# Attention backward on one core: E is transposed in groups of six in every step, and the dK/dV matmuls move to step 19, behind those transposes

## The chip, the core and the metric

The kernel runs on one core of a Trainium2 chip. The metric is device time in microseconds (us) for one execution. Before the change three runs took 2691.83, 2700.37 and 2707.21 us, so the median is 2700.37 us.

## The reference

The reference computes one block `x + s * g` and all its gradients. There, `s` is multi-head attention on a normalised `x` (32 heads of 16 channels, 2048 tokens), and `g` is a gated channel MLP. Only the attention matters for this change:

```python
xn  = layernorm(A_x)
q, k, v = split_heads(xn @ wqkv)            # 32 heads, 16 channels, 2048 tokens
p   = softmax(q k^T / 4)                    # 2048 x 2048 for every head
o   = p v ;  s = o @ wo
out = x + s * silu(mlp(xn))
grads = vjp(out, grad_out)                  # of A_x, A_wqkv, A_wo and the MLP's weights
```

The backward pass of the attention needs, for every head, dV = P^T dO, dS = P * (dO V^T - rowsum), dQ = dS K and dK = dS^T Q. The kernel never stores P. It computes E = exp(scores - bound) once, and G = (V dO^T) * E, and corrects for the softmax's sum and for the row sums afterwards.

## The kernel before

The program has three phases: layer norms, projections and MLP forward (`phase_pre`), the attention with its backward pass (`attention_core`, about 284 to 2084 us of the profiled span), and the remaining gradients (`phase3`). The change touches only `attention_core`.

**Tiling.** Heads are taken in 16 pairs, and queries in four chunks `qc` of 512, which makes 64 blocks. A block has 16 steps `kb`, one for every 128 keys. There are thus 1024 steps, numbered g, and a loop of 24 more to drain. "Step 10" below means g mod 16 = 10. A queue order is written out by hand: every engine executes its instructions in the order in which the body of the loop over g emits them (`tc.manual_schedule()`).

**What one step does**, with the tile names that the profile uses:

- `emit_s(g + 1, hj)`: scores `s` of the next step, one matmul for each head of the pair (L629), and on ScalarE their exponential into the tile `et` (L635), which holds E with keys on the partitions, four steps to a tile.
- `emit_d(g, hj)`: the products `d` of V and dO (L647).
- `emit_mult(g)`: on VectorE, `gts` = `d` times `et`, which is G (L660), two instructions of 128x512.
- `emit_x(g - 1, "l" / "e" / "g")`: six narrow matmuls into the accumulator `X` (L719, L722, L725): sums of E, E against K and V, and G against ones and K.
- `emit_dmat(g)`: DMA transposes on SyncE's queue (SP). In every second step one turns `gts` into `gk` (queries on the partitions), and in every fourth one turns a quarter of `et` (the query sub-block `qb` = 3 of four steps) into `ek`.
- `emit_T` and `emit_cT`: the other three quarters of E. In 12 of 16 steps TensorE transposes eight 128x128 blocks of an `et` tile that was completed earlier into the PSUM tile `tT` (L694), and ScalarE copies them to `ek` (L704).
- `emit_z` and `emit_acc`: four matmuls of 32 output rows into the accumulator `Z`, which becomes dK and dV of 1024 keys (L804). Their stationary operands `W1`, `W2` hold corrected Q and dO. A block has 16 such units, one a step; they run from the 21st step after its first (`ZOFF = -21`), eight for each half of the keys. After eight units the half is added to `acc` by VectorE (L817 for the first query chunk, L819 for the others). This falls on steps 12 and 4.
- Once in a block: `emit_xs` copies `X` to SBUF on ScalarE (L734) in step 0 of the next block. `emit_XT` transposes it in fp32 on TensorE (L744) and `emit_fin` (VectorE L756 to L770, then GpSimd) makes `W1`, `W2`, O and dQ of it in step 2 (`FIN_AT = 2`).

**Order in a step.** TensorE gets `Z`, the first `s`, (`XT` in step 2), both `d`, the second `s`, `tT`, and the `X` matmuls of the step before. ScalarE gets two exponentials, (`xs` in step 0), and the copy of `tT`. VectorE gets (`acc`), the two products, (`fin`).

**Buffers.** `s` and `tT` share a ring of three PSUM banks (`ps_st`), `d` and `XT` another of three (`ps_d`). `X` and `Z` have one bank each. In SBUF there are three tiles of `et`, three of `gts`, seven of `gk` and nineteen of `ek`. A matmul into a ring's bank waits until the reader of the bank's last content has finished.

Of the kernel before, what the change touches and what calls it, by code (L numbers as in the profile page):

```python
# [8 lines left out]
bf16 = mybir.dt.bfloat16  # L9
f32 = mybir.dt.float32  # L10
# [532 lines left out]
def attention_core(ctx, tc, NAT_s, NATQ_s, Oall, dQall, dKVT_out, ident_f32, ident_bf, npairs=16, nqc=4):  # L543
    nc = tc.nc
# [5 lines left out]
    ps_z = ctx.enter_context(tc.tile_pool(name="ps_z", bufs=1, space=PSUM))  # L550
    etp = sb("etp", 3)
    gtp = sb("gtp", 3)
    gbp = sb("gbp", 7)
    ekp = sb("ekp", 19)
    xsp = sb("xsp", 1)
    finp = sb("finp", 1)
    wp = sb("wp", 2)
# [49 lines left out]
    cur = {}  # L607

    def a_unit(g):
        return (g // 16, g % 16) if 0 <= g < NSTEP else None  # L610
# [53 lines left out]
    def emit_dmat(g):  # L664
        a = a_unit(g)
        if a is None:
            return
        j, kb = a
        kc = kb // 4
        if kb % 2 == 1:  # L670
            h = (kb // 2) % 2
            if h == 0:
                blk[j]["Gk"][kc] = gbp.tile([128, 2, 16, 128], bf16, name="gk")
            nc.sync.dma_start_transpose(out=blk[j]["Gk"][kc][:, h], in_=st_gt[g][:].rearrange("k a h q -> k (a h q)"))
        if kb % 4 == 3:
            ek = ekp.tile([128, 8, 128], bf16, name="ek")
            blk[j]["Ek"][(kc, 3)] = ek
            nc.sync.dma_start_transpose(out=ek[:], in_=st_et[g][:, 3].rearrange("k a h q -> k (a h q)"))

    def t_unit(g):  # L680
        a = a_unit(g - 4)
        if a is None or a[1] % 4 == 3:
            return None
        return a[0], a[1] // 4, a[1] % 4

    def emit_T(g):
        u = t_unit(g)
        if u is None:
            return
        j, kc, qb = u  # L690
        et = st_et[j * 16 + kc * 4 + 3]
        t = ps_st.tile([128, 8, 128], bf16, name="tT", tag="st")
        for b in range(8):
            nc.tensor.transpose(t[:, b, :], et[:, qb, b // 2, b % 2, :], ident_bf[:])  # L694
        st_T[g] = t

    def emit_cT(g):
        u = t_unit(g)
        if u is None:
            return  # L700
        j, kc, qb = u
        ek = ekp.tile([128, 8, 128], bf16, name="ek")
        blk[j]["Ek"][(kc, qb)] = ek
        nc.scalar.copy(out=ek[:].rearrange("q a k -> q (a k)").bitcast(f32),  # L704
                       in_=st_T.pop(g)[:].rearrange("q a k -> q (a k)").bitcast(f32))

    def emit_x(g, part):
        a = a_unit(g)
# [19 lines left out]
    def emit_xs(g):  # L728
        a = a_unit(g)
        if a is None or a[1] != 15:  # L730
            return
        j = a[0]
        xs = xsp.tile([128, 512], f32, name="xs")
        nc.scalar.copy(out=xs[:], in_=blk[j].pop("X")[:])  # L734
        blk[j]["xs"] = xs

# [10 lines left out]
    def emit_fin(g):  # L747
        j = g // 16 - 1
        if g % 16 != FIN_AT or not 0 <= j < NB:
            return  # L750
        p, qc = blocks[j]
        NQq = op_of(j)["NATQq"]
        NQd = op_of(j)["NATQd"]
        XT = blk[j].pop("XT")
        xt = finp.tile([128, 4, 128], f32, name="xt")
        nc.vector.tensor_copy(out=xt[:], in_=XT[:])  # L756
        XTv = xt[:].rearrange("q b (r c) -> q b r c", r=4)
        W1 = wp.tile([128, 4, 2, 32], bf16, name="W1")
        W2 = wp.tile([128, 4, 2, 32], bf16, name="W2")
        nc.gpsimd.memset(W2[:, :, :, 0:16], 0.0)  # L760
        st0 = qc * 4
        nqs = NQq[:, st0:st0 + 4, :, 1:17]
        ndo = NQd[:, st0:st0 + 4, :, :]
        bc = lambda ap: ap.to_broadcast([128, 4, 2, 16])
        rL = finp.tile([128, 4, 2, 1], f32, name="rL")
        nc.vector.reciprocal(out=rL[:], in_=XTv[:, :, 2:4, 17:18])  # L766
        dl = finp.tile([128, 4, 2, 1], f32, name="dl")
        nc.vector.tensor_tensor(out=dl[:], in0=XTv[:, :, 2:4, 0:1], in1=rL[:], op=ALU.mult)
        ndr = finp.tile([128, 4, 2, 1], f32, name="ndr")
        nc.vector.scalar_tensor_tensor(out=ndr[:], in0=dl[:], scalar=-1.0, in1=rL[:], op0=ALU.mult, op1=ALU.mult)  # L770
        nc.gpsimd.tensor_tensor(out=W2[:, :, :, 16:32], in0=nqs, in1=bc(rL[:]), op=ALU.mult)  # L771
        nc.gpsimd.tensor_tensor(out=W1[:, :, :, 0:16], in0=ndo, in1=bc(rL[:]), op=ALU.mult)
        nc.gpsimd.tensor_tensor(out=W1[:, :, :, 16:32], in0=nqs, in1=bc(ndr[:]), op=ALU.mult)
        Ov = Oall[:, st0:st0 + 4, p * 32:(p + 1) * 32].rearrange("q b (h c) -> q b h c", h=2)
        nc.gpsimd.tensor_tensor(out=Ov, in0=XTv[:, :, 0:2, 16:32], in1=bc(rL[:]), op=ALU.mult)
        t1 = finp.tile([128, 4, 2, 16], f32, name="t1")
        nc.gpsimd.tensor_tensor(out=t1[:], in0=XTv[:, :, 0:2, 0:16], in1=bc(dl[:]), op=ALU.mult)
        nc.gpsimd.tensor_tensor(out=t1[:], in0=XTv[:, :, 2:4, 1:17], in1=t1[:], op=ALU.subtract)
        rL4 = finp.tile([128, 4, 2, 1], f32, name="rL4")
        nc.gpsimd.tensor_scalar(out=rL4[:], in0=rL[:], scalar1=0.25, scalar2=None, op0=ALU.mult)  # L780
        dQv = dQall[:, st0:st0 + 4, p * 32:(p + 1) * 32].rearrange("q b (h c) -> q b h c", h=2)
        nc.gpsimd.tensor_tensor(out=dQv, in0=t1[:], in1=bc(rL4[:]), op=ALU.mult)
        blk[j]["W1"] = W1
        blk[j]["W2"] = W2

    def emit_z(g):
        u = z_unit(g)
        if u is None:
            return
        j, kp, qb, part = u  # L790
        if part == 0 and qb == 0:
            blk[j]["Z"] = ps_z.tile([128, 512], f32, name="Z", tag="z")
        Z = blk[j]["Z"]
        for par in range(2):
            kc = 2 * kp + par
            if part == 0:
                W = blk[j]["W2"]
                mv = blk[j]["Gk"][kc][:].rearrange("q a (r h b) k -> q h b a r k", r=2, h=2)[:, :, qb]
            else:
                W = blk[j]["W1"]  # L800
                mv = blk[j]["Ek"].pop((kc, qb))[:].rearrange("q (a h) k -> q h a k", h=2)
            for hj in range(2):
                r = 64 * par + 32 * hj
                nc.tensor.matmul(Z[r:r + 32, :], lhsT=W[:, qb, hj, :], rhs=mv[:, hj],  # L804
                                 start=(part == 0 and qb == 0), stop=(part == 1 and qb == 3), skip_group_check=True,
                                 tile_position=(0, r))

    def emit_acc(g):
        u = z_unit(g)
        if u is None or u[2] != 3 or u[3] != 1:  # L810
            return
        j, kp = u[0], u[1]
        p, qc = blocks[j]
        Z = blk[j]["Z"]
        av = acc[:, kp, :]
        if qc == 0:
            nc.vector.tensor_copy(out=av, in_=Z[:])  # L817
        else:
            nc.vector.tensor_tensor(out=av, in0=Z[:], in1=av, op=ALU.add)  # L819
        if qc == nqc - 1:  # L820
            if kp == 0:
                cur["ob"] = outp.tile([128, 2, 512], bf16, name="ob")
            ob = cur["ob"]
            nc.gpsimd.tensor_copy(out=ob[:, kp, :], in_=av)
            if kp == 1:
                def store():
                    dv = dKVT_out[p * 64:(p + 1) * 64, :].rearrange("r (a b s) -> r a b s", a=2, b=2)
                    for b in range(2):
                        nc.sync.dma_start(out=dv[:, :, b, :], in_=ob[b * 64:(b + 1) * 64])
                late.append((cur["g"] + 2, store))  # L830

    FIN_AT = 2
    ZOFF = -21
    late = []
    for f in load_ops(0):
        f()
# [2 lines left out]
    for g in range(NSTEP + 16 + 8):  # L839
        cur["g"] = g  # L840
        a = a_unit(g)
        if a is not None:
            j, kb = a
            p, qc = blocks[j]
            if kb == 0 and qc == 1 and p + 1 < npairs:
                for i, f in enumerate(load_ops(p + 1)):
                    late.append((g + 1 + 4 * i, f))
        for it in [x for x in late if x[0] <= g]:
            late.remove(it)
            it[1]()  # L850
        emit_z(g + ZOFF)
        emit_acc(g + ZOFF)
        emit_s(g + 1, 0)
        emit_XT(g)
        emit_d(g, 0)
        emit_d(g, 1)
        emit_s(g + 1, 1)
        emit_mult(g)
        emit_fin(g)
        emit_T(g)  # L860
        emit_x(g - 1, "l")
        emit_x(g - 1, "e")
        emit_x(g - 1, "g")
        emit_xs(g - 1)
        emit_cT(g)
        emit_dmat(g)
        st_gt.pop(g - 2, None)
        st_et.pop(g - 12, None)
# [104 lines left out]
```

## Time and profile before

| | |
|---|---|
| median of three runs | 2700.37 us (2691.83 to 2707.21) |
| the profiled execution: time, span | 2689.98 us, 2688.2 us |
| mean granted TensorE clock | 0.957 of full speed |
| share of the span busy: PE, VectorE, ScalarE, GpSimd | 85%, 71%, 67%, 22% |
| in the attention (284 to 2084 us): PE, VectorE, ScalarE, GpSimd | 1702.7, 1433.8, 1529.8, 249.3 us of 1800 |
| granted clock and DMA share in that stretch | 1.00, 1.08 |
| transposes `tT` (L694) | 6144, 475.2 us busy |
| copies of `tT` (L704) | 768, 455.2 us busy, mean 593 ns |

The page lists busy time by engine (PE is TensorE's matmuls, PEld its weight loads, DVE is VectorE, ACT ScalarE, POOL GpSimd, SP SyncE). Matmuls are pipelined: each is shown for some 0.38 us here, though the next may begin 0.22 us after it or at the same time, so a busy engine is not one at its peak. More is learned from the timeline, which gives the start and length of every instruction, and in brackets how long its engine had been idle and what ended that. A DMA share above 1 means that several packets overlap on an engine.

### The profile page before, as it was taken

What the parts mean: (1) busy time and instruction counts of PE and PEld (TensorE: products, weight loads), DVE (VectorE), ACT (ScalarE), POOL (GpSimd) and SP (SyncE); (2) the same over time, 40 slices, a digit from 0 to 9 for tenths busy, and PEclk for the clock granted to TensorE, in tenths of its full rate; (3) what the DMA queues carried; (4) which work ended last, traced back from release to release, by engine and by line L of the source; (5) the groups of instructions that cost most, each with busy time, mean ns of one, the idle gap of its engine ahead of it and who ended that gap; (6) DMA issues with size and microseconds to landing.
All of it is one profiled execution on the core that took longest, in us unless ns stands there. A gap on an engine that the chain in (4) does not pass through costs nothing. (4 is left out here: it accounts for less than half of the span.)

```text
span 2688.2 us, 61100 instructions
## 1 busy us (share of the span) xinstructions
PE 2294.1 (85%) x24005; PEld 1054.0 (39%) x24064; DVE 1898.4 (71%) x3190; ACT 1795.7 (67%) x3317; POOL 600.7 (22%) x990
## 2 busy tenths in 40 slices
PE   3788799999999999999999999999999656656967
PEld 2333244444444444444444444444444333322433
DVE  5766687878788778787787877778787368860144
ACT  3344688888888888888888888888887254430110
POOL 0434111011110111101111011110111258850034
PEclk8899899999999999999999999999999878878989
DMA  5343999999999999999999999999999633327331
GB/s 188 94 128 126 186 199 212 195 211 204 204 216 193 211 204 204 215 196 215 201 202 215 191 214 202 205 209 198 210 198 182 229 109 103 103 72 185 116 111 43
DMA packets 1564740, 477.08 MB, mean 177 GB/s; under 512 B 1484706, under 2 KB 1549603, under 8 KB 1564451
## 3 DMA queue, kind: packets, MB, share of 16 engines
q1 hardware_dynamic: 1491058, 419.56, 78.5%
q10 hardware_dynamic: 73392, 53.62, 6.5%
q8 instruction: 188, 3.08, 0.5%
q14 instruction: 102, 0.83, 0.1%
HBM read 65.41 MB, written 55.32 MB: 45 GB/s over the span
## 5 line engine op out<-in xcount | busy, mean ns | idle before, releaser
L660 DVE TENSOR_TENSOR gts<-d,et 128x512 bf16<-128x512 f32 x2048 | 1292.3, 683 | 364.1 <-PE s L629 200.1
L635 ACT ACTIVATE et<-s 128x512 bf16<-128x512 f32 x2048 | 1127.3, 596 | 247.9 <-PE s L629 136.7
L629 PE MATMUL s<-QDT,KVT 32*128 32x512 bf16 x2048 | 528.0, 386 | 17.7 <-DMA QDT<-Pad 16.1
L647 PE MATMUL d<-QDT,KVT 32*128 32x512 bf16 x2048 | 489.9, 383 | 54.0 <-DVE gts L660 53.7
L694 PE MATMUL tT<-ident_bf,et 128*128 128x128 bf16 x6144 | 475.2, 220 | 40.1 <-ACT ek L704 39.4
L704 ACT COPY ek<-tT 128x512 f32<-128x512 f32 x768 | 455.2, 593 | 0.5 <-PE tT L694 0.5
L694 PEld LDWEIGHTS <-et 128*128 128x128 bf16 x6144 | 354.2, 98 | 213.1 <-issue 199.2
L722 PE MATMUL X<-et,NAT 128*32 128x512 bf16 x2048 | 404.0, 392 | 0.0
L719 PE MATMUL X<-et,Lc 128*32 128x512 bf16 x2048 | 403.4, 391 | 0.0
L725 PE MATMUL X<-gts,NAT 128*17 128x512 bf16 x2048 | 393.4, 380 | 0.0
L629 PEld LDWEIGHTS <-KVT 32*128 32x128 bf16 x2048 | 145.3, 91 | 555.1 <-issue 523.8
L804 PE MATMUL Z<-ek,W 128*32 128x512 bf16 x2048 | 300.8, 380 | 0.0
L804 PE MATMUL Z<-gk,W 128*32 128x512 bf16 x2048 | 289.6, 380 | 1.3 <-DVE acc L819 1.3
L771 POOL TENSOR_TENSOR W<-NATQq,rL 128x128 bf16<-128x128 bf16 x64 | 25.7, 401 | 1178.3 <-DVE rL L766 1178.3
L804 PEld LDWEIGHTS <-W 128*32 128x32 bf16 x4096 | 199.7, 96 | 125.9 <-issue 31.2
L719 PEld LDWEIGHTS <-Lc 128*32 128x32 bf16 x2048 | 98.2, 93 | 139.0 <-issue 59.6
L647 PEld LDWEIGHTS <-KVT 32*128 32x128 bf16 x2048 | 96.0, 91 | 11.4 <-issue 11.4
L722 PEld LDWEIGHTS <-NAT 128*32 128x32 bf16 x2048 | 98.6, 93 | 0.0
L421 PE MATMUL dh_tp<-ident_bf,dh 128*128 128x128 bf16 x224 | 31.0, 278 | 77.9 <-DVE dh L418 75.5
L725 PEld LDWEIGHTS <-NAT 128*17 128x17 bf16 x2048 | 95.3, 90 | 0.0
L448 PE MATMUL ps_dw<-dm_all,hgc 128*128 128x512 bf16 x220 | 54.0, 402 | 29.6 <-DMA hgc<-HG_s 29.4
L427 PE MATMUL ps_dy<-w1T,dh1T 128*128 128x512 bf16 x208 | 67.8, 471 | 3.7 <-ACT dh1T L422 3.4
(197 smaller groups left out, 2442.2 us busy)
## 6 DMA issues: line engine op xcount, KB each, us to landing
gk<-gts SPq DMA_TRANSPOSE x512, 4.2
HG_s<-hg SPq DMA_DIRECT2D x16, 448.0 KB, 2.9
DH_s<-dh ACTq DMA_DIRECT2D x16, 448.0 KB, 2.5
NAT<-NAT_s SPq DMA_DIRECT2D x16, 264.0 KB, 3.3
GB_s<-gB ACTq DMA_DIRECT2D x16, 256.0 KB, 2.0
ek<-et SPq DMA_TRANSPOSE x256, 3.1
dKVT_s<-ob SPq DMA_DIRECT2D x32, 128.0 KB, 2.5
dhc<-DH_s ACTq DMA_DIRECT2D x2, 2048.0 KB, 13.7
```

The costliest lines, as they stand in the source:

```text
L427: nc.tensor.matmul(ps[:], lhsT=dh1T[:, fc, :], rhs=w1T[:, fc, :], start=(fc == 0), stop=(fc == FC - 1))
L448: nc.tensor.matmul(ps[:], lhsT=hgc[:, t, :], rhs=dm_all[:, t, :], start=(t == 0), stop=(t == NT - 1))
L629: nc.tensor.matmul(s[:], lhsT=op["KVT"][r:r + 32, kb * 128:(kb + 1) * 128], rhs=op["QDT"][r:r + 32, qc * 512:(qc + 1) * 512], start=True, ...
L635: nc.scalar.activation(out=et[:, :, kb % 4, hj, :], in_=s[:].rearrange("k (b q) -> k b q", b=4), func=ACT.Exp)
L647: nc.tensor.matmul(d[:], lhsT=op["KVT"][r:r + 32, kb * 128:(kb + 1) * 128], rhs=op["QDT"][r:r + 32, qc * 512:(qc + 1) * 512], start=True, ...
L660: nc.vector.tensor_tensor(out=gts[:, kb % 2, hj, :].rearrange("k (b q) -> k b q", b=4), in0=st_d.pop((g, hj))[:].rearrange("k (b q) -> k b ...
L694: nc.tensor.transpose(t[:, b, :], et[:, qb, b // 2, b % 2, :], ident_bf[:])
L704: nc.scalar.copy(out=ek[:].rearrange("q a k -> q (a k)").bitcast(f32), in_=st_T.pop(g)[:].rearrange("q a k -> q (a k)").bitcast(f32))
L719: nc.tensor.matmul(X[64 + 32 * hj:96 + 32 * hj, :], lhsT=Lc[:], rhs=et[:, :, kb % 4, hj, :], start=(kb == 0), stop=False, skip_group_check ...
L722: nc.tensor.matmul(X[32 * hj:32 * hj + 32, :], lhsT=NATt[:, kb, hj, 1:33], rhs=et[:, :, kb % 4, hj, :], start=(kb == 0), stop=(kb == 15), ...
L725: nc.tensor.matmul(X[64 + 32 * hj:64 + 32 * hj + 17, :], lhsT=NATt[:, kb, hj, 0:17], rhs=st_gt[g][:, kb % 2, hj, :], start=False, stop=(kb ...
L804: nc.tensor.matmul(Z[r:r + 32, :], lhsT=W[:, qb, hj, :], rhs=mv[:, hj], start=(part == 0 and qb == 0), stop=(part == 1 and qb == 3), skip_ ...
```

## The change

Three things change in `attention_core`, with the buffers that they need.

1. The transposes. In all 16 steps of a block TensorE transposes six 128x128 blocks of E, those of the current step (three query sub-blocks of both heads), instead of eight blocks of an older tile in 12 of 16 steps. ScalarE copies 128x384 words each time. One `ek` tile of four steps is filled by four such copies.
2. The order. `Z` is no longer first in the step. It stands behind the transposes, and in step 1 behind `XT`, and before the `X` matmuls. `XT` moves from between `s` and `d` to behind the transposes. dK/dV of a block begin at its step 19 instead of 21, so `acc` falls on steps 10 and 2, and `fin` is done in step 1 instead of 2.
3. Buffers: `gk` six tiles instead of seven, `ek` six small (from the DMA) and six large (from ScalarE) instead of nineteen small, and `xt` uses the buffer of `xs`. The output tile `ob` is stored after each half instead of after both, in stores of half the size.

```diff
-    gbp = sb("gbp", 7)
-    ekp = sb("ekp", 19)
+    gbp = sb("gbp", 6)
+    ekd = sb("ekd", 6)
+    ekc = sb("ekc", 6)
...
-    def t_unit(g):
-        a = a_unit(g - 4)
-        if a is None or a[1] % 4 == 3:
-            return None
-        return a[0], a[1] // 4, a[1] % 4
...
     def emit_T(g):
-        u = t_unit(g)
-        if u is None:
-            return
-        j, kc, qb = u
-        et = st_et[j * 16 + kc * 4 + 3]
-        t = ps_st.tile([128, 8, 128], bf16, name="tT", tag="st")
-        for b in range(8):
-            nc.tensor.transpose(t[:, b, :], et[:, qb, b // 2, b % 2, :], ident_bf[:])
+        a = a_unit(g)
+        if a is None:
+            return
+        kk = a[1] % 4
+        et = st_et[g]
+        t = ps_st.tile([128, 3, 2, 128], bf16, name="tT", tag="st")
+        for qb in range(3):
+            for hj in range(2):
+                nc.tensor.transpose(t[:, qb, hj, :], et[:, qb, kk, hj, :], ident_bf[:])
         st_T[g] = t
 
     def emit_cT(g):
...
-        ek = ekp.tile([128, 8, 128], bf16, name="ek")
-        blk[j]["Ek"][(kc, qb)] = ek
-        nc.scalar.copy(out=ek[:].rearrange("q a k -> q (a k)").bitcast(f32),
-                       in_=st_T.pop(g)[:].rearrange("q a k -> q (a k)").bitcast(f32))
+        if kk == 0:
+            cur["ek"] = ekc.tile([128, 3, 4, 2, 128], bf16, name="ek")
+            blk[j]["Ek"][kc] = cur["ek"]
+        nc.scalar.copy(out=cur["ek"][:, :, kk].rearrange("q b h k -> q b (h k)").bitcast(f32),
+                       in_=t[:].rearrange("q b h k -> q b (h k)").bitcast(f32))
...
-        xs = xsp.tile([128, 512], f32, name="xs")
+        xs = xsp.tile([128, 512], f32, name="xs", tag="xs")
...
-        xt = finp.tile([128, 4, 128], f32, name="xt")
+        xt = xsp.tile([128, 4, 128], f32, name="xt", tag="xs")
...
-    FIN_AT = 2
-    ZOFF = -21
+    FIN_AT = 1
+    ZOFF = -19
...
-        emit_z(g + ZOFF)
-        emit_acc(g + ZOFF)
         emit_s(g + 1, 0)
-        emit_XT(g)
         emit_d(g, 0)
         emit_d(g, 1)
         emit_s(g + 1, 1)
+        emit_T(g)
+        emit_XT(g)
+        emit_z(g + ZOFF)
+        emit_acc(g + ZOFF)
         emit_mult(g)
         emit_fin(g)
-        emit_T(g)
         emit_x(g - 1, "l")
```

More of the change, by code (lines that the diff above doesn't have):

```diff
@@ L675, in emit_dmat @@
         if kb % 4 == 3:
-            ek = ekp.tile([128, 8, 128], bf16, name="ek")
+            ek = ekd.tile([128, 4, 2, 128], bf16, name="ekd")
             blk[j]["Ek"][(kc, 3)] = ek
-            nc.sync.dma_start_transpose(out=ek[:], in_=st_et[g][:, 3].rearrange("k a h q -> k (a h q)"))
-    def t_unit(g):
-        a = a_unit(g - 4)
-        if a is None or a[1] % 4 == 3:
-            return None
-        return a[0], a[1] // 4, a[1] % 4
+            nc.sync.dma_start_transpose(out=ek[:].rearrange("q a h k -> q (a h) k"), in_=st_et[g][:, 3].rearrange("k a h q -> k (a h q)"))
     def emit_T(g):
-        u = t_unit(g)
-        if u is None:
+        a = a_unit(g)
+        if a is None:
             return
-        j, kc, qb = u
-        et = st_et[j * 16 + kc * 4 + 3]
-        t = ps_st.tile([128, 8, 128], bf16, name="tT", tag="st")
-        for b in range(8):
-            nc.tensor.transpose(t[:, b, :], et[:, qb, b // 2, b % 2, :], ident_bf[:])
+        kk = a[1] % 4
[4 more added lines that the diff above has]
+                nc.tensor.transpose(t[:, qb, hj, :], et[:, qb, kk, hj, :], ident_bf[:])
         st_T[g] = t
     def emit_cT(g):
-        u = t_unit(g)
-        if u is None:
+        a = a_unit(g)
+        if a is None:
             return
-        j, kc, qb = u
-        ek = ekp.tile([128, 8, 128], bf16, name="ek")
-        blk[j]["Ek"][(kc, qb)] = ek
-        nc.scalar.copy(out=ek[:].rearrange("q a k -> q (a k)").bitcast(f32),
-                       in_=st_T.pop(g)[:].rearrange("q a k -> q (a k)").bitcast(f32))
+        j, kb = a
+        kc, kk = kb // 4, kb % 4
+        t = st_T.pop(g)
+        if kk == 0:
[3 more added lines that the diff above has]
+                       in_=t[:].rearrange("q b h k -> q b (h k)").bitcast(f32))
     def emit_x(g, part):
@@ L800, in emit_z @@
                 W = blk[j]["W1"]
-                mv = blk[j]["Ek"].pop((kc, qb))[:].rearrange("q (a h) k -> q h a k", h=2)
+                mv = blk[j]["Ek"][(kc, 3)][:] if qb == 3 else blk[j]["Ek"][kc][:, qb]
+                mv = mv.rearrange("q a h k -> q h a k")
             for hj in range(2):
@@ L820, in emit_acc, with store @@
         if qc == nqc - 1:
[L821 to L830, printed above, removed]
-    FIN_AT = 2
-    ZOFF = -21
+            ob = outp.tile([128, 512], bf16, name="ob")
+            nc.gpsimd.tensor_copy(out=ob[:], in_=av)
+            def store():
+                dv = dKVT_out[p * 64:(p + 1) * 64, :].rearrange("r (a b s) -> r a b s", a=2, b=2)
+                for b in range(2):
+                    nc.sync.dma_start(out=dv[:, kp, b, :], in_=ob[b * 64:(b + 1) * 64, :])
+            late.append((cur["g"] + 2, store))
+    FIN_AT = 1
+    ZOFF = -19
     late = []
```

## The prediction

> **What bounds the kernel now.** I read the page first, then the busy time of the attention by windows, then the timeline of one block engine by engine, and last ScalarE's groups by form.
>
> ```profile
> PE 2294.1 (85%) x24005; PEld 1054.0 (39%) x24064; DVE 1898.4 (71%) x3190; ACT 1795.7 (67%) x3317; POOL 600.7 (22%) x990
> ```
>
> In the attention TensorE is busy 1702.7 of 1800 us, at a granted clock of 1.00. That looks like a TensorE bound, but its matmuls overlap, so what counts is when each may start. TensorE in step 0 of a block, in the steps after it, and in step 4:
>
> ```profile
> 1010.53 0.38 PE L629 MATMUL s<-QDT,KVT 32*128 32x512 bf16 x1
> 1010.85 0.62 PE L694 MATMUL tT<-ident_bf,et 128*128 128x128 bf16 x8
> 1011.40 0.39 PE L719 MATMUL X<-et,Lc 128*32 128x512 bf16 x2
> ...
> 1011.62 0.38 PE L725 MATMUL X<-gts,NAT 128*17 128x512 bf16 x2
> 1011.63 0.59 PE L804 MATMUL Z<-gk,W 128*32 128x512 bf16 x4
> 1012.15 0.39 PE L629 MATMUL s<-QDT,KVT 32*128 32x512 bf16 x1
> ...
> 1013.20 0.61 PE L694 MATMUL tT<-ident_bf,et 128*128 128x128 bf16 x8 [0.65 <-ACT ek L704]
> ...
> 1014.81 0.66 PE L744 MATMUL XT<-ident_f,xs 128*128 128x128 f32 x4
> 1015.40 0.39 PE L647 MATMUL d<-QDT,KVT 32*128 32x512 bf16 x2
> ...
> 1019.23 0.37 PE L647 MATMUL d<-QDT,KVT 32*128 32x512 bf16 x1 [0.54 <-DVE gts L660]
> ```
>
> From these starts: scores to transposes 0.32; eight transposes 0.55 (0.068 each); first `X` to its third matmul 0.22; first `X` to the next scores 0.75 (with `Z`); `XT` 0.59. A packed step is 1.63 with eight transposes and 1.08 without. The two brackets are the two ways of losing time: the bank of `tT` is still being copied, or the bank of `d` is still being multiplied. ScalarE and VectorE around the same places:
>
> ```profile
> 1010.87 1.09 ACT L635 ACTIVATE et<-s 128x512 bf16<-128x512 f32 x2 [0.51 <-PE s L629]
> 1012.07 0.59 ACT L734 COPY xs<-X 128x512 f32<-128x512 f32 x1
> 1012.56 0.59 ACT L704 COPY ek<-tT 128x512 f32<-128x512 f32 x1
> ...
> 1027.61 1.08 ACT L635 ACTIVATE et<-s 128x512 bf16<-128x512 f32 x2 [0.25 <-PE s L629]
> 1028.58 0.59 ACT L704 COPY ek<-tT 128x512 f32<-128x512 f32 x1
> ```
>
> ```profile
> 1017.08 0.68 DVE L756 COPY xt<-XT 128x512 f32<-128x512 f32 x1
> ...
> 1018.50 1.27 DVE L660 TENSOR_TENSOR gts<-d,et 128x512 bf16<-128x512 f32 x2
> 1019.69 0.68 DVE L817 COPY acc<-Z 128x512 f32<-128x512 f32 x1
> 1020.29 2.47 DVE L660 TENSOR_TENSOR gts<-d,et 128x512 bf16<-128x512 f32 x4
> ```
>
> Two exponentials take 0.97 until the copy begins (1027.61 to 1028.58). The scores of that step began at 1027.19, so 0.42 passes before the exponential, and the first product began at 1027.71, 0.52 after `d`. On VectorE one product follows another after 0.60 (each ends 0.685 after its start), `acc` holds up the next product by 0.60, and the `fin` chain by 1.42. One undisturbed block lasts from 1011.40 to 1038.99 (`X` of step 0 to `X` of the next step 0), 27.59 us.
>
> **The plain step.** The count of transposes stays at 6144 (16 x 6 a block for 12 x 8); they are only spread evenly. Six take 6 x 0.068 = 0.41, and `Z` moved to the other side of `X` leaves 0.75 to the next scores, since the order is only rotated among narrow matmuls. Packed TensorE: 0.41 + 0.75 + 0.32 = 1.48, against a mean of (12 x 1.63 + 4 x 1.08) / 16 = 1.49. So TensorE gains nothing. The copy shrinks. From these two rows, for 512 and 256 words,
>
> ```profile
> L704 ACT COPY ek<-tT 128x512 f32<-128x512 f32 x768 | 455.2, 593 | 0.5 <-PE tT L694 0.5
> L538 ACT CAST ob_kv<-ps_dwkv 128x256 bf16<-128x256 f32 x8 | 3.0, 373 | 90.3 <-DVE ob_kv L537 90.3
> ```
>
> I take the middle, 0.48, for 384 words (bounds: 0.37 and 0.59). 1024 such copies are 492 us busy against 455, beside TensorE. What matters is the loop: transposes, scores of two steps on, exponentials, copy, and the bank is free for the transposes two steps on. After: 0.41 + 0.75 + 0.42 + 0.97 + 0.48 + 0.05 (copy's end to transposes, 1013.15 to 1013.20) = 3.08 for two steps, 2 x 1.54. Since TensorE alone needs 1.48, intervals alternate between 1.48 and 1.60. Before, four steps without `acc` or `fin` (steps 8 to 11, `X` at 1024.61 to 1030.84) took 6.23; after 6.16. The even spread is thus worth 4 x 0.07 = 0.28 us a block.
>
> The Trainium skill, "ScalarE: Activation LUTs", Rules for kernel authors, budgets about 0.3 us for each ACTIVATE and 0.83 ns for each element, which speaks against 256 more instructions. The rows agree on the slope (0.213 us for 256 words) and give a fixed part of 0.16, not 0.3. By the page the copy would be an estimated 0.62 and the sum some 50 us higher.
>
> **`acc` behind the transposes.** This is the price. Before, `Z` was first in the step, so `acc` found it finished: in step 12 `X` to `X` is 1.82 and in step 13 1.79, against 1.82 and 1.63 in steps 8 and 9. After, count from the start of the transposes of step 10. `Z` starts at 0.41, VectorE sees it 0.52 later, at 0.93. The products of step 10, whose `d` were ready at 0.20, stand behind `acc` on VectorE: first product at 1.53, ended at 2.22, bank free at 2.28 (0.06 later, as the bracket at 1019.23 shows). The second `d` of step 11 needs that bank (ring of three) and was due at 1.17: 1.11 lost, and the second scores and the transposes queue behind it. The interval is 1.48 + 1.11 = 2.59. Nothing covers it: the ring has one spare bank, and it is used up by 1.17.
>
> That VectorE's queue lets nothing overtake is stated in the Trainium skill, "PSUM — Partial Sum Buffer", Engine vs sequencer instructions (strict FIFO). No row of before shows a product waiting behind an `acc` that itself waits; if one could overtake, both stalls would go and the sum would be some 130 us lower.
>
> **`xs`, `XT`, `fin`, `acc` in steps 0 to 2.** Count from the transposes of step 0. The last `X` matmul begins at 0.41 + 0.22 (`Z`) + 0.22 = 0.85, `xs` 0.45 later (1011.62 to 1012.07) at 1.30, the copy 0.49 later at 1.79, ended at 2.27; transposes of step 1 at 2.32. (Before: 2.35.) Then `XT` at 2.73, `Z` at 3.32, scores at 4.07, transposes of step 2 at 4.39: an interval of 2.07. VectorE begins `xt` at 3.44 and is free at 4.86. `Z` of step 2 is seen at 4.39 + 0.41 + 0.52 = 5.32, so `acc` waits again, and the interval is 2.59 as above. `fin` itself costs TensorE only the 0.59 of `XT`; the work of GpSimd on `W1`, `W2` ends near 5.7, covered until `Z` of step 3 at 7.39.
>
> **Things I cost at nothing.** Copies of steps 0 and 8 also wait for `Z` of their step (six large `ek`), seen at 0.93; the exponentials end the engine's work at 1.07, so they hide it, and without that cover it would be 0.4 twice a block. `gk` transposes of steps 9 and 1 wait on SP for `Z` (six tiles), but they wait longer for the products. With them on SP stand 32 more stores in 16 pairs, 0.6 each to issue (1.20 for two, row L829): 0 to 19 us, taken as 0, since SP mostly waits for VectorE (869.9 us on L660).
>
> **The sum.** A block has the intervals 2.32, 2.07, 2.59, 2.59 and 12 plain ones. After a disturbance ScalarE is ahead, so seven are 1.48 and five 1.60. Total 9.57 + 18.36 = 27.93. Rules of this kind fall short of the trace by 0.02 in waited intervals (1.80 for a measured 1.82), five times: 28.03. Against 27.59 this is +0.44 a block, for 62 blocks with all parts (the first has no `fin` or `acc`) +27 us. Once in a pair a product waits for a `gk` transpose behind the operand loads (step 15, 21 us in all): steps 10 to 14 grow from 8.03 to 8.63, which gives back up to 15 x 0.6 = 9, while steps 2 to 6 shrink by 0.57 and may add up to that again; I take -5. Two `Z` units less in the drain: -1 (0.22 each, with waits). Sum **+21 us**. The profiled execution, 2690, would be 2711; against the median, 2700.4, I forecast **2721**. By itself this case spans 2705 (stall 0.1 shorter, -12, and DMA at -9) to 2745 (copy 0.05 longer, 0.05 x 6 x 62 = 19, and DMA at 0).
>
> **Rivals.** *No change* (2702): the stalls at `acc` are 0.95 instead of 1.11 (2 x 0.16 x 62 = 20), which the even spread just pays. *Faster*: `acc` costs what it does now, 0.16 in steps 12 and 13, because products in reserve keep `d` going. This would take off 2 x 0.95 x 62 = 118, to 2603; the point from which it turns to faster by 0.5% is a stall under 0.83. For it speaks that VectorE is only 80% busy, against it the bracket at 1019.23: one late product stops `d` at once. I place that side at half the saving, 2662. *Much slower* (2762): a copy of 384 words costs as much as one of 512, 0.11 x 6 a block x 62; against it speaks the row of 256.
>
> **Chances.** Half a per cent (13.5 us) is about what the measurement tells from no change; the three runs alone span 15. Faster 0.15, within it 0.25, slower 0.6, of which the much slower case holds 0.08. The range 2672 to 2764 leaves out half of the faster case and the tail of the much slower.
>
> **What would show it.** Right: `gts` waits after `acc` on PE `Z`, twice a block; `d` waits for `gts` some 1.1 us in the same steps; transposes in plain steps at 1.48 and 1.60; copies near 0.48. Wrong: `acc` starting without idle time, plain intervals over 1.6, or `gk` transposes in front of products at new places.

## The result and the profile after

The changed kernel takes 2725.47 us (median of five runs, 2722.65 to 2729.98), the kernel before 2694.38 in the same session. The ratio is 1.0108, with a 95% interval of 1.0079 to 1.0137. So it is slower, by about 29 us by the ratio (the medians differ by 31). Run again beside the experiments, on another occasion, it gave 2725.19 and 1.0102 (1.0083 to 1.0121). The profiled execution has a span of 2728.2 us at a granted clock of 0.953.

Three groups of the page of after, with busy time and mean, and then the idle time before them and what ended it; below them the groups of `d` and `acc` of before:

```profile
L648 PE MATMUL d<-QDT,KVT 32*128 32x512 bf16 x2048 | 454.7, 387 | 99.3 <-DVE gts L661 99.3
L703 ACT COPY ek<-tT 128x384 f32<-128x384 f32 x1024 | 496.6, 485 | 0.6 <-PE tT L690 0.5
...
L819 DVE TENSOR_TENSOR acc<-Z,acc 128x512 f32<-128x512 f32 x96 | 66.4, 691 | 64.3 <-PE Z L804 64.3
```

```profile
L647 PE MATMUL d<-QDT,KVT 32*128 32x512 bf16 x2048 | 489.9, 383 | 54.0 <-DVE gts L660 53.7
L819 DVE TENSOR_TENSOR acc<-Z,acc 128x512 f32<-128x512 f32 x96 | 65.1, 678 | 2.0 <-PE Z L804 2.0
```

`d` now waits 99.3 us for products, where it waited 53.7 before. `acc` waited 2.0 us for `Z` before, and now 64.3. The copies take 485 ns and wait for next to nothing (0.6 us in all), also where they need `Z` to free a large `ek` tile: that cover held.

The timeline of TensorE around the transposes of step 10 (1392.90), step 11 (1395.47) and step 12 (1397.00) of one block of after:

```profile
1392.56 0.39 PE L648 MATMUL d<-QDT,KVT 32*128 32x512 bf16 x2
...
1392.90 0.49 PE L690 MATMUL tT<-ident_bf,et 128*128 128x128 bf16 x6
1393.32 0.40 PE L804 MATMUL Z<-ekd,W 128*32 128x512 bf16 x4
...
1393.56 0.38 PE L718 MATMUL X<-et,Lc 128*32 128x512 bf16 x2
...
1394.09 0.39 PE L648 MATMUL d<-QDT,KVT 32*128 32x512 bf16 x1
1395.15 0.38 PE L648 MATMUL d<-QDT,KVT 32*128 32x512 bf16 x1 [0.67 <-DVE gts L661]
...
1395.47 0.51 PE L690 MATMUL tT<-ident_bf,et 128*128 128x128 bf16 x6
...
1397.00 0.51 PE L690 MATMUL tT<-ident_bf,et 128*128 128x128 bf16 x6
```

And VectorE at the same time:

```profile
1393.80 0.69 DVE L819 TENSOR_TENSOR acc<-Z,acc 128x512 f32<-128x512 f32 x1 [1.02 <-PE Z L804]
1394.41 2.47 DVE L661 TENSOR_TENSOR gts<-d,et 128x512 bf16<-128x512 f32 x4
```

Both `d` of step 10 start at 1392.56, and a product may start some 0.52 later, at 1393.08. But VectorE sits idle for 1.02 us: next in its queue is `acc`, which waits for the `Z` that started at 1393.32. The first product follows at 1394.41, ends at 1395.10, and the second `d` of step 11 starts at 1395.15 instead of 1394.09. That is 1.06 us, and TensorE's whole queue stands behind it. The next interval of the transposes, 1.53, is a plain one.

To compare kernels I use two numbers taken from the timeline. The *undisturbed block* is the sum, over the 16 steps, of the median time from one `X` start to the next (over blocks 4 to 63). The *excess* is the time from the first `X` start of the attention to the last, less 64 such blocks. In the excess are the waits that fall only in some blocks. As starts are read to 0.01 us, it is good to about 2 us. Before: 27.59 and 21 us. After: 28.19 and 21, in the second profile 28.20 and 13. What lies outside the attention is 898 to 904 us in all profiles, so the whole difference is made there.

### The profile page after: what moved, and what is told of

It is laid out like the page before. It is cut to its first block, busy times and chain, and to the rows that moved or that the text cites. A ratio compares the mean times of both kernels' runs of the same rounds, so it can differ in the third digit from the quotient of the medians.

```text
span 2728.2 us, 61404 instructions
## 1 busy us (share of the span) xinstructions
PE 2288.5 (84%) x24064; PEld 1029.0 (38%) x24064; DVE 1931.4 (71%) x3190; ACT 1805.4 (66%) x3573; POOL 599.8 (22%) x990
## 5 line engine op out<-in xcount | busy, mean ns | idle before, releaser
L690 PE MATMUL tT<-ident_bf,et 128*128 128x128 bf16 x6144 | 515.5, 220 | 50.3 <-ACT ek L703 50.2
L648 PE MATMUL d<-QDT,KVT 32*128 32x512 bf16 x2048 | 454.7, 387 | 99.3 <-DVE gts L661 99.3
L703 ACT COPY ek<-tT 128x384 f32<-128x384 f32 x1024 | 496.6, 485 | 0.6 <-PE tT L690 0.5
L630 PE MATMUL s<-QDT,KVT 32*128 32x512 bf16 x2048 | 464.3, 385 | 17.9 <-DMA QDT<-Pad 16.3
L690 PEld LDWEIGHTS <-et 128*128 128x128 bf16 x6144 | 369.4, 97 | 288.5 <-issue 273.8
L630 PEld LDWEIGHTS <-KVT 32*128 32x128 bf16 x2048 | 115.2, 91 | 477.0 <-issue 476.9
L804 PE MATMUL Z<-gk,W 128*32 128x512 bf16 x2048 | 205.0, 390 | 1.4 <-DVE acc L819 1.4
L804 PE MATMUL Z<-ek,W 128*32 128x512 bf16 x1536 | 154.6, 392 | 0.0
L648 PEld LDWEIGHTS <-KVT 32*128 32x128 bf16 x2048 | 107.2, 91 | 125.2 <-DVE gts L661 124.7
L804 PEld LDWEIGHTS <-W 128*32 128x32 bf16 x4096 | 105.2, 93 | 112.2 <-issue 13.6
L819 DVE TENSOR_TENSOR acc<-Z,acc 128x512 f32<-128x512 f32 x96 | 66.4, 691 | 64.3 <-PE Z L804 64.3
```

Of the source, the lines that this page charges most:

```text
L630: nc.tensor.matmul(s[:], lhsT=op["KVT"][r:r + 32, kb * 128:(kb + 1) * 128], rhs=op["QDT"][r:r + 32, qc * 512:(qc + 1) * 512], start=True, ...
L648: nc.tensor.matmul(d[:], lhsT=op["KVT"][r:r + 32, kb * 128:(kb + 1) * 128], rhs=op["QDT"][r:r + 32, qc * 512:(qc + 1) * 512], start=True, ...
L690: nc.tensor.transpose(t[:, qb, hj, :], et[:, qb, kk, hj, :], ident_bf[:])
L703: nc.scalar.copy(out=cur["ek"][:, :, kk].rearrange("q b h k -> q b (h k)").bitcast(f32), in_=t[:].rearrange("q b h k -> q b (h k)").bitcas ...
```

## The experiments

Three theories stood at the start. A: the products stand behind an `acc` that waits for `Z`. B: finer copies and their loop are the loss. C: the six `gk` tiles and the DMA transposes are. Two more came later, on what the excess is. D: products wait until a `gk` transpose has read the buffer of `gts` that they are to overwrite, so the buffers are too few. E: the transposes themselves are the limit. What came out, in order of the block (in us, as the excess):

| kernel | block | excess | median | ratio to before, same session (95%) |
|---|---|---|---|---|
| before with `Z` behind the transposes (c_zback) | 29.67 | -4 | 2795.64 | 1.0394 (1.0378 to 1.0409) |
| changed, copies in two (h_two, one run) | 28.56 | 10 | 2740.48 | |
| changed, again (after_again) | 28.20 | 13 | 2725.19 | 1.0102 (1.0083 to 1.0121) |
| before, four `gts` (j_before4) | 27.65 | -4 | 2669.67 | 0.9908 (0.9893 to 0.9923) |
| changed, `xs` behind the copy (d_xs) | 27.60 | 29 | 2694.55 | 1.0022 (1.0011 to 1.0033) |
| before, `XT` behind the transposes (l_xt) | 26.72 | 48 | 2659.36 | 0.9873 (0.9855 to 0.9892) |
| changed, `acc` behind the products (a_acc) | 26.72 | 53 | 2664.86 | 0.9912 (0.9895 to 0.9929) |
| changed, `Z` at the head (b_zfirst) | 26.49 | 56 | 2654.52 | 0.9870 (0.9854 to 0.9887) |
| the same, `xs` behind the copy (f_zfirst_xs) | 26.17 | 79 | 2653.55 | 0.9832 (0.9809 to 0.9856) |
| the same, without the operand loads of pairs 2 to 15 (i_noload) | 26.17 | 8 | 2585.06 | 0.9590 (0.9572 to 0.9608) |
| f_zfirst_xs, four `gts` (g_gts4) | 26.18 | 30 | 2614.35 | 0.9689 (0.9660 to 0.9717) |
| before, three edits (n_all) | 26.03 | 20 | 2594.17 | 0.9629 (0.9610 to 0.9649) |

**The changed kernel once more.** It is the reference for the others of its session.

> The changed kernel as it is, on the same chip as the next ones. Its attention takes 1825 us by its trace against 1787 before, 38 more, while the ratio of the runs, 1.0108, says 29. Expected: 1.010 to 1.015, 2715 to 2728; blocks of 28.19 where nothing waits for a transfer, and about 20 us over 64 of these.

It came out as expected. Its excess of 13 against 21 shows how much the rare waits differ between two executions of one kernel, and that accounts for most of the gap between the first profile (38 us more than before in the attention) and the runs (29).

**`acc` behind the products.**

```diff
-            emit_acc(g + ZOFF)
             emit_mult(g)
+            emit_acc(g + ZOFF)
```

> The changed kernel, with `acc` emitted behind the two products of its step on VectorE instead of in front of them; nothing else differs. Theory A (the products stand behind an `acc` that waits for `Z`, so a bank of `d` comes free late): the two intervals of 2.58 shrink to about 1.7 and 1.9, a block from 28.19 to 26.6, 62 x 1.6 = 98 us less than the changed kernel, about 2627 (0.975 of before); `d` no longer waits for `gts` in these steps. Part of it may come back as waits of products for `gk` transposes. Rival B (the finer copies and their loop make the change slower): the plain intervals of 1.53 and 1.59 are its cost, `acc` is only where it shows; under 15 us gained, 2710 or more. Rival C (six `gk` tiles and the DMA transposes): no gain, since these are untouched.

The two intervals of 2.58 became 2.00 (step 3, with `fin`) and 1.69 (step 11); the block is 26.72, where 26.6 was expected. They are not quite plain, as `Z` now waits for `acc` to free its one bank (`PE Z L804 <- DVE acc L819: 16.5, 48, 0.4` in the list of waits: total, times, longest). VectorE in this kernel, in step 10 of the same block:

```profile
1352.99 1.29 DVE L661 TENSOR_TENSOR gts<-d,et 128x512 bf16<-128x512 f32 x2 [0.29 <-ACT ek L703]
1354.20 0.68 DVE L819 TENSOR_TENSOR acc<-Z,acc 128x512 f32<-128x512 f32 x1
1354.80 2.70 DVE L661 TENSOR_TENSOR gts<-d,et 128x512 bf16<-128x512 f32 x4
```

The products come first, `acc` finds `Z` finished and has no idle time before it. This one line is worth 62 x 1.47 = 91 us of undisturbed blocks and carries the kernel from 1% slower to 0.9% faster than before. B and C can't explain that, as copies, buffers and transfers are the same, nor can TensorE's clock: it is 0.99 in the attention of both kernels (1.00 before). But only some 53 to 62 us arrive, as the excess rises from 13 or 21 to 53.

**`Z` back at the head of the step.**

```diff
+        emit_z(g + ZOFF)
+        emit_acc(g + ZOFF)
         emit_s(g + 1, 0)
...
-        emit_z(g + ZOFF)
-        emit_acc(g + ZOFF)
         emit_mult(g)
```

> The changed kernel, with `Z` and `acc` back at the head of the step, as before the change; transposes, buffers, steps 19 and 1 stay as changed. Theory A: `acc` finds `Z` finished, both intervals of 2.58 become plain ones of 1.5 to 1.6 (2.1 with `fin`), a block takes 26.4, 62 x 1.8 = 112 us less than the changed kernel, about 2613 (0.970 of before). Then six transposes in every step are by themselves a gain of about 80 us over before. Rival B: the six-wise transposes and copies are the loss, so the kernel stays over 2700. Rival C: no gain.

Again the block is as expected (26.49 against 26.4) and the time 41 us above, with an excess of 56. The rest of the change, without its order of `Z`, is thus a gain of 1.3% over before.

**The order alone, in the kernel before.**

```diff
-        emit_z(g + ZOFF)
-        emit_acc(g + ZOFF)
         emit_s(g + 1, 0)
...
         emit_s(g + 1, 1)
+        emit_T(g)
+        emit_z(g + ZOFF)
+        emit_acc(g + ZOFF)
         emit_mult(g)
         emit_fin(g)
-        emit_T(g)
```

> The kernel before, with `Z` and `acc` moved behind the transposes (in the four steps of a block that have none, behind the scores); eight transposes in 12 of 16 steps, steps 21 and 2 and all buffers stay. Theory A: with eight transposes ahead, `Z` is seen later still, so steps 4 and 12 lose about 1.0 each in the interval after them, a block goes from 27.6 to 29.8, 62 x 2.2 = 136 us more, about 2830 (1.05 of before). Rivals B and C: this order alone changes nothing, within 10 us of 2694.

It costs 2.08 a block, 62 x 2.08 = 129 us, and 107 of them show. The excess falls from 21 to nothing, and products wait 4.4 us for `gk` transposes in its list of waits, against 29.7 before: it seems that slower steps leave the transfers more time. VectorE in step 12, and TensorE in step 13, look as in the changed kernel; the second `d` is due beside the first, at 1432.54:

```profile
1432.25 0.69 DVE L819 TENSOR_TENSOR acc<-Z,acc 128x512 f32<-128x512 f32 x1 [0.81 <-PE Z L804]
```

```profile
1432.54 0.38 PE L647 MATMUL d<-QDT,KVT 32*128 32x512 bf16 x1
1433.60 0.39 PE L647 MATMUL d<-QDT,KVT 32*128 32x512 bf16 x1 [0.67 <-DVE gts L660]
```

**`xs` behind the copy.**

```diff
-        emit_xs(g - 1)
         emit_cT(g)
+        emit_xs(g - 1)
```

> The changed kernel, with the copy of `X` (`xs`) in step 0 emitted behind the copy of the transposes on ScalarE instead of in front of it. The step that I put at 2.32 (transposes of step 1 wait until `xs`, which waits for the last `X` matmul, and then the copy are through) should become plain: 28.19 to 27.5 a block, 62 x 0.68 = 42 us less than the changed kernel, about 2683 (0.996 of before). If the wait in step 1 is due to something else (`XT`, the bank of `d`), nothing changes: 2725.

The interval of step 1, from `X` to `X`, went from 2.84 to 2.24, the block from 28.2 to 27.60. From transposes to transposes, 2.40 became a plain 1.59, so the wait was what I took it for. The next such interval grew from 1.96 to 2.17, as `XT` now waits for the later `xs` (its weight loads 11.3 us in all, 1.3 in the changed kernel): that is why 0.60 were gained and not 0.68. Also here part of it came back in the excess.

**Copies cut in two.**

```diff
-        nc.scalar.copy(out=cur["ek"][:, :, kk].rearrange("q b h k -> q b (h k)").bitcast(f32),
-                       in_=t[:].rearrange("q b h k -> q b (h k)").bitcast(f32))
+        for b0, b1 in ((0, 2), (2, 3)):
+            nc.scalar.copy(out=cur["ek"][:, b0:b1, kk].rearrange("q b h k -> q b (h k)").bitcast(f32),
+                           in_=t[:, b0:b1].rearrange("q b h k -> q b (h k)").bitcast(f32))
```

> The changed kernel with every copy of the transposes cut in two, of 256 and 128 words. The loop of transposes, scores, exponentials and copy should get longer by the fixed part of one more instruction, 0.16, in two steps: 1.53 and 1.59 become 1.53 and 1.70 or so, a block goes from 28.19 to 28.8, about 38 us more. If TensorE alone sets the plain step, nothing changes.

The groups by form of this kernel, and one pair of copies in the timeline:

```profile
L704 ACT COPY ek<-tT 128x256 f32<-128x256 f32 x1024 | 388.0, 379 | 0.6 <-PE tT L690 0.5
L704 ACT COPY ek<-tT 128x128 f32<-128x128 f32 x1024 | 303.0, 296 | 0.0
```

```profile
1405.33 0.55 ACT L704 COPY ek<-tT 128x256 f32<-128x256 f32 x2
```

Every second plain interval grew, from 1.59 to 1.65, and the others stayed at 1.53. So the loop through ScalarE is there and alternates as counted, but a second copy that follows the first directly adds only 0.06 to it, not 0.16. The two instructions overlap: the pair takes 0.55 from start to end, 0.06 more than the one copy of 0.485, and not 0.379 + 0.296. The rise of 15 us over the changed kernel is from one run.

**Where the gains went.** The next four ask about the excess. The first is the kernel with `Z` at the head and the edit of d_xs:

> The changed kernel with `Z` and `acc` at the head of the step and with `xs` behind the copy of the transposes. An undisturbed block goes from 26.49 (`Z` at the head alone) to 26.2, 62 x 0.3 = 19 us, which gives 2636 (0.980). Theory D (what the earlier versions failed to gain, 50 to 60 us over 64 undisturbed blocks against 21, went into products that wait for `gk` transposes before they may overwrite `gts`): the waits grow by some 10 us, and 2645 is more likely. If they were due to the place of `Z`, they stay at 56.

0.32 a block were gained, 20 us, but the excess went from 56 to 79: nothing is left of it in the profile, and some 10 us in the runs (0.9832 against 0.9870). The waits are in its list of waits (400 to 2000 us: total, times, longest):

```profile
DVE gts L661 <- DMA gk<-gts: 71.4, 44, 4.5
```

The same line for this kernel with `gtp = sb("gtp", 4)`:

```profile
DVE gts L661 <- DMA gk<-gts: 32.9, 22, 3.9
```

> The kernel with `Z` at the head and `xs` behind the copy, and a fourth buffer of `gts`. Theory D, with the ring of `gts` as what makes the products wait: a product may run two steps (3 us) further ahead of the DMA transposes, longest waits seen were 3.5, so the excess over 64 undisturbed blocks falls from 56 or more to under 20, and the time to about 2600 (0.967). Rival E: the transposes themselves are the limit (the DMA engines are busy all the time): then a longer ring only moves the wait, and less than 10 us are gained over the same kernel with three.

39 us were gained, between what D and E expected. What is left sits further on, in steps 1 and 9 instead of 15, 7 and 11: a fourth buffer postpones the wait and absorbs much of it, and the backlog of the transfers is real. With three buffers most of the excess, some 64 of 79 us, falls in the second block of a pair, in which the operands of the next pair are loaded. The next kernel has three buffers and leaves out the operand loads of pairs 2 to 15 (`if kb == 0 and qc == 1 and p + 1 < 2`), so these pairs compute with the operands of pairs 0 and 1:

> The kernel with `Z` at the head, `xs` behind the copy and three buffers of `gts`, without the operand loads of pairs 2 to 15: these pairs compute with the operands of pairs 0 and 1, and everything else is done in full. Theory D, as sharpened by the fourth buffer: the transposes `KVT` and `QDT` of the next pair stand in SP's queue before `gk`, and what follows waits. Without them the excess of 79 us over 64 undisturbed blocks of 26.17 falls under 15, and the time to about 2590 (0.960). If the `gk` and `ek` transposes alone are too much at this pace, products keep waiting in all four blocks of a pair and the excess stays over 40.

```profile
DVE gts L661 <- DMA gk<-gts: 7.2, 9, 1.1
```

The excess is 8, and the time is the one expected, within 5 us. So what eats the gains is the load of the next pair, which stands before `gk` in SP's queue; at this pace `gk` and `ek` alone still keep up. A load is three plain transfers and two transposes, with copies on GpSimd between them. Which of these costs most is not shown, as the run leaves out all of them.

In the kernel before, the fourth buffer (with `xt` in the buffer of `xs` to make room) does the same:

> The kernel before, with a fourth buffer of `gts` (room comes from `xt` in the buffer of `xs`). Its undisturbed blocks stay at 27.59, its excess of 21 us over 64 of them falls to under 5: 2675 (0.993). A rival to theory D, that step 15 waits for something else in the load of a pair, expects no gain.

No wait of products for `gk` is left in its list, where before has 29.7 us, and the excess is gone.

**`XT` alone.**

```diff
         emit_s(g + 1, 0)
-        emit_XT(g)
...
         emit_s(g + 1, 1)
+        emit_T(g)
+        emit_XT(g)
         emit_mult(g)
         emit_fin(g)
-        emit_T(g)
```

> The kernel before, with `XT` alone moved from between the scores and `d` to behind the transposes, still in step 2. Expected from the starts in the trace: step 2 goes from 2.54 to 2.2, steps 3 and 4 from 3.83 together to 3.3, since the products of step 2 no longer wait for `XT`; a block from 27.59 to 26.75, 62 x 0.85 = 53 us less, of which products waiting for `gk` may take a half back: 2640 to 2665 (0.98 to 0.99). If the place of `XT` doesn't matter and only `Z` does, 2690.

Step 2 takes 2.08, steps 3 and 4 3.42, the block 26.72. Of the gain of 1.10 a block that the change brings with `Z` at the head (27.59 to 26.49), the place of `XT` alone gives 0.87, and in time the two kernels are alike (0.9873 and 0.9870). It is the useful part of the change. At the same block of 26.72, this kernel with seven `gk` tiles has an excess of 48, and a_acc with six has 53, so of theory C little is left in the excess either.

**Eight or six.** The kernel before with `XT` behind the transposes, `xs` behind the copy and four `gts` (again with `xt` in the buffer of `xs`):

> The kernel before, with eight transposes in 12 of 16 steps, `Z` at the head and steps 21 and 2, and three edits: `XT` behind the transposes, `xs` behind the copy, four buffers of `gts`. My count of six against eight transposes gave the even spread 0.28 a block, 17 us. With the other waits gone here too, an undisturbed block should take 26.1 to 26.3, as much as with six (26.17), so the spread is worth 0 to 10 us and the time is 2600 to 2625 (0.965 to 0.975). If the even spread matters by itself, this kernel stays 20 us or more behind the one with six.

The block is 26.03 and the time 2594.17, 3.7% under before and the fastest of those that compute everything. With the same waits removed, six transposes in every step (g_gts4) take 26.18 and 2614. The two also differ in the steps of dK/dV and `fin`, in the tiles of `gk` and `ek` and in the stores of `ob`, so the spread isn't measured alone; but no gain from it shows.

## Why the prediction was right

**The decisive step held.** I had `Z` seen 0.52 after its start (measured 0.48), the first product at 1.53 after the transposes (1.51), the second `d` 1.11 late (1.06), and intervals of 2.59 (2.58). a_acc and b_zfirst take this away, c_zback puts it into the kernel before, and each moves the block by what the same count gives. The rival on the faster side, that products in reserve hide the wait, is refuted: the bank of `d` is missed at once. The much slower rival fell with the copy's 485 ns, next to the 0.48 taken from the rows for 512 and 256 words. The fixed 0.3 us of the Trainium skill's page ("ScalarE: Activation LUTs", Rules for kernel authors) stand there for an ACTIVATE whose bias is a pointer operand, and with them the copy would be an estimated 0.62. These copies are written without a bias, so that budget is not theirs, and the measurement decides.

**`xs`, `XT` and `fin`.** From transposes to transposes, as I counted, the intervals that begin in steps 0, 1, 2 and 10 take 2.40, 1.96, 2.58 and 2.57, together 9.51; I had 2.32, 2.07, 2.59 and 2.59, together 9.57. The sum is closer than its first two parts, and that is luck. TensorE and ScalarE from step 0 to step 2, 10 us behind the rows of step 10 above:

```profile
1403.25 0.49 PE L690 MATMUL tT<-ident_bf,et 128*128 128x128 bf16 x6
...
1405.64 0.49 PE L690 MATMUL tT<-ident_bf,et 128*128 128x128 bf16 x6 [0.81 <-ACT ek L703]
1405.97 0.61 PE L743 MATMUL XT<-ident_f,xs 128*128 128x128 f32 x4
1406.51 0.40 PE L804 MATMUL Z<-gk,W 128*32 128x512 bf16 x4
...
1407.60 0.51 PE L690 MATMUL tT<-ident_bf,et 128*128 128x128 bf16 x6
```

```profile
1404.63 0.59 ACT L733 COPY xs<-X 128x512 f32<-128x512 f32 x1 [0.22 <-PE X L724]
1405.11 0.48 ACT L703 COPY ek<-tT 128x384 f32<-128x384 f32 x1
```

`xs` begins 1.38 after the transposes of step 0, where I had 1.30, so the transposes of step 1 come 0.08 later. `XT` is shown to start 0.33 after them and not 0.41, and holds TensorE for 0.54 instead of 0.59, so this interval is 0.43 longer than a plain one, where I had 0.59. `fin` costs nothing beyond it, as said: step 11, without `fin`, has the same 2.58 from `X` to `X` as step 3.

**The mis-sized term is the plain step.** From `X` to `X`, twelve intervals are plain, seven of 1.53 and five of 1.59: 18.66. I had seven of 1.48 and five of 1.60, with 0.02 added to the long ones: 18.46. One of the seven begins in step 15:

```profile
1401.71 0.50 PE L690 MATMUL tT<-ident_bf,et 128*128 128x128 bf16 x6
1402.14 0.40 PE L804 MATMUL Z<-gk,W 128*32 128x512 bf16 x4
...
1402.90 0.39 PE L630 MATMUL s<-QDT,KVT 32*128 32x512 bf16 x1
```

On the median the six transposes take 0.43 to 0.44 to the next matmul instead of 0.41, the way from there to the next scores 0.76 instead of 0.75, and from the scores to the transposes 0.33 to 0.34 instead of 0.32. The first of these is a mistake of scaling. In both kernels the transposes of a group start 0.056 apart, and 0.15 pass from the last start to the next matmul; I divided the 0.55 of eight by eight and so shrank the 0.15 too. Four plain steps now take 6.24, against 6.23 before, so nothing is left of the 0.28 a block that I gave to the even spread. The block was 28.19 to my 28.03, so the undisturbed blocks lost 62 x 0.60 = 37 us, not 27.

**The transfers** gave back nothing in one profile (an excess of 21 as before) and 8 us in the other (13); I had 5, with bounds of -9 and 0. So 21 us were forecast and some 29 measured in both sessions. The block adds 62 x 0.16 = 10 us to the forecast, nearly all of it in the plain step, and the transfers of the second profile take 3 off. That the forecast of 2721 lies only 4 us from the measured 2725 is in part luck: it stood on a median of 2700.37, and the five runs of before have 2694.38.

**What I had not counted on** is how much of a change in pace the transfers take back. Counting starts gave every block of the experiments within 0.25 us, but the times of the first four were off by 12 to 41 us. With D in the expectation (f_zfirst_xs, g_gts4, i_noload, j_before4 and l_xt) the later ones were off by 14 at most. h_two, expected without it, cost 15 us more than the changed kernel instead of 38, and n_all came 6 us under its range.

## What to carry to other kernels

On an engine that executes in order, an instruction that waits costs what stands behind it; so ask of every moved producer who waits for it, and put that consumer behind the work whose inputs are ready sooner. Here one line on VectorE decided between 1% slower and 0.9% faster. Count a change in two parts, the step that repeats and the rare waits for shared transfers: when the step got shorter here, the second part grew, and a buffer more in the ring that the transfers release gained 39 us, where the last improvement of the step had gained 10.

## What was unexpected

Two copies in a row on ScalarE cost less than the sum of their durations: 379 and 296 ns in place of one of 485, for 0.06 us more in the loop. And the kernel reaches a pace at which nearly the same transfers that left 21 us of waits at 27.6 us a block leave 79 at 26.2, with three buffers of `gts`.
